# Zero matmuls between the first loads and the first scores of a block-sparse attention kernel

## The chip, the cores and the metric

The kernel runs on one core of a Trainium2 chip. The metric is the device time of one execution in microseconds (us). The core has five engines that are used here, each with its own instruction queue that it works through in order: TensorE (PE in the profile; its weight loads are listed apart as PEld), VectorE (DVE), ScalarE (ACT), GpSimd (POOL) and SyncE (SP), which issues most DMAs. [...]

## The reference

Attention with a block mask, and a two-layer network behind it. Batch 4, 8 heads, 768 positions, head size 64; the mask has blocks of 32.

```python
scores = scale * np.matmul(q, k.transpose(0, 1, 3, 2))
# mask: neighbours, first and last block row and column, 3 sampled blocks per row
scores = np.where(mask, scores, -1000000000.0)
attn = np.exp(scores - np.max(scores, axis=-1, keepdims=True))
attn = attn / (np.sum(attn, axis=-1, keepdims=True) + 1e-09)
x = np.matmul(attn, v)      # then (3072 tokens, 512)
h = x @ w_in                # (512, 2048)
g = h * (1.0 / (1.0 + np.exp(-beta * h)))
out = g @ w_out             # (2048, 512)
```

## The kernel before, in words

Everything is computed in 16-bit floats on TensorE with 32-bit accumulation in PSUM. The heads are taken in pairs (16 pairs, four per batch entry), and a unit is one pair with 256 or 512 query rows. For a unit the kernel needs k and q of the pair, turned so that the head's 64 values lie on the partitions (`kX`, `qX`), and v with a column of ones (`va`). k, q and v come in by DMA as 32-bit floats (`st_k`, `st_q`, `st_v`), are cast by DVE or POOL (`s_k`, `s_q`, `va`), and for the first four pairs turned by TensorE transposes against `identity`; DVE or ACT copies the result out of PSUM to `kX` and `qX`. The first pair's k is loaded in three parts, each cast and turned by itself.

A score step writes a buffer `sc` of two PSUM banks: two heads side by side, in the upper and the lower half of the array's rows, which run at the same time as a pair. In the first four units the mask is added on TensorE: before each pair of score matmuls a pair `sc<-shut_qk,onehot` puts a large negative number where the mask is shut. `shut_qk` is made by ACT out of the mask matmul (`sc<-identity,mask`), which reads `mask`, made by DVE from the sampled blocks. ACT then takes the exponential of the 128x1024 scores (`et<-sc`), in later units DVE multiplies it with a 0/1 mask, and 24 matmuls of 65 columns (`sc<-va,et`) multiply with v. DVE divides by the sum, and the result is turned for the network: `sc<-x,w_in_sb` (h), tanh on ACT (`t_sb`), the gate on DVE (`g`), and products with `w_out_sb`.

There are eight PSUM banks, four double buffers `T["sc"][0..3]`; a buffer of the pool `mm` is one bank of them, numbered 0 to 7, so bank 4 and bank 5 are the two halves of `T["sc"][2]`. The class `Banks` keeps record of who touches which half, and declares instructions of different engines independent where they touch different halves.

The order of all work is written out in `STEPS`: each word is a node's number, a letter for its engine (P TensorE, A ScalarE, D VectorE, G GpSimd, S SyncE) and the slots of the buffers that it takes. `in_steps` (line 157) turns the text into the list `seq`, and the loop at the end of the kernel emits one node after the other; instructions of one engine are queued in that order. The words that matter here: `11S0`, `19S`, `23S` load the three parts of the first k, `12G0` casts the first part, `13P0` turns it (two transposes into bank 0); `25P1`, `17P2` and `21P3` turn the third part, the first q and the second part; `1P4` is the mask matmul into bank 4, `9P0` the transpose of beta, `2A` makes `shut_qk`, `80P3`, `82P2` and `84P1` are the three score steps of unit 0, `81A0`, `83A1`, `85A2` their exponentials. `91P2`, `93P3` and `95P2` are the score steps of unit 1, `86P1` the product with v of unit 0. `54D0` and `50D3` cast q and k of the fourth pair (unit 3), `56A` copies its `qX`.

Before the list begins, `emit_first` sets up constants (among them `warm`, 512 columns of zeros in the buffer that later holds `g`), and ends with `emit_warm(4)`: four matmuls of 512 columns of zeros against zeros, whose result nobody reads. In the profile they stand under line 297; nearly everything else that is emitted through the recording helper stands under line 180.

## Time and profile before

| | |
|---|---|
| median of 3 runs | 271.65 us (271.62 to 271.89) |
| profiled execution | 270.99 us, of which the span from first to last instruction is 269.2 |
| TensorE busy | 257.1 us, 96% of the span |
| VectorE, ScalarE, GpSimd busy | 224.5, 212.6, 24.9 us |
| moved by DMA | 36.67 MB, mean 136 GB/s; some 290 GB/s between 4 and 18 us |

A line of the timeline reads: start in us from the start of the span, duration of the group in us, engine, source line, operation, output and input by the program's names, shapes, number of instructions, and in brackets the idle time of the engine before it and what ended that. Matmuls overlap, and their durations hold the way through the array, so the time that a matmul costs is read from the distance between starts. The chain lists, back from the last instruction, what released each step; shown here in order of time, with start, duration and what it was.

### The profile page before, as it was taken

The numbers are of one execution on the slowest core, as the hardware profiler recorded it, in microseconds if no ns is written. First come the engines' busy times: TensorE is split into PE (matmuls) and PEld (weight loads), VectorE is DVE, ScalarE is ACT, GpSimd is POOL, SyncE is SP. The second block draws the span as 40 slices with busy tenths as digits, with TensorE's granted clock in tenths as the row PEclk, the third lists the DMA queues.
The fourth block names the chain that finished last, engine by engine and source line by source line (L and its number), as shares of the span: only waits on it lengthen the run. The fifth ranks groups of instructions, "written<-read, shape, count | busy, mean of one in ns | idle before, by whom it ended". The sixth has DMA issues, their size and how long they took to land.

```text
span 269.2 us, 6710 instructions
## 1 busy us (share of the span) xinstructions
PE 257.1 (96%) x2719; PEld 163.0 (61%) x2719; DVE 224.5 (83%) x480; ACT 212.6 (79%) x288; POOL 24.9 (9%) x39
## 2 busy tenths in 40 slices
PE   4899799999999999999999999999999999999993
PEld 1576565554453755447776547755467885568883
DVE  6364599889999898989999899878999896898381
ACT  1779999889999796988798699888769678774231
POOL 4170001001110000000021001611000000000000
PEclk9999999999999999999999999999999999999999
DMA  6999996589955487973663079865006010220042
GB/s 183 292 260 213 210 225 186 120 206 227 237 149 150 125 205 143 194 178 105 180 158 57 0 205 225 151 170 46 0 4 195 4 22 2 88 97 2 2 156 78
DMA packets 72881, 36.67 MB, mean 136 GB/s; under 512 B 29828, under 2 KB 68756, under 8 KB 72852
## 3 DMA queue, kind: packets, MB, share of 16 engines
q1 hardware_dynamic: 69600, 32.06, 50.1%
q0 software_dynamic: 3136, 4.19, 8.8%
q8 instruction: 21, 0.34, 0.6%
q14 instruction: 8, 0.07, 0.1%
q10 hardware_dynamic: 116, 0.01, 0.0%
HBM read 27.27 MB, written 6.29 MB: 125 GB/s over the span
## 4 chain that ended last, share of the span: by engine, by line
PE 86%; ACT 5%; DVE 5%; issue 1%; DMA 1%; SPq 1%; POOL 0%; DVEq 0%; ACTq 0%
PE sc L180 86%; ACT et L180 4%; DVE et L180 2%; DVE g L180 1%; DMA st_k<-in_k_dram 1%; ACT t_sb L180 1%; SPq L478 1%; DVE qX L180 0%; DVE kX L180 0%; ACT shut_qk L180 0%; DVE s_k L180 0%; POOL s_k L504 0%; ACT osb L180 0%; ACT qX L180 0%; DVE recip L180 0%
## 5 line engine op out<-in xcount | busy, mean ns | idle before, releaser
L180 ACT ACTIVATE et<-sc 128x1024 f16<-128x1024 f32 x144 | 141.6, 1057 | 17.8 <-PE sc L180 17.1
L180 PE MATMUL sc<-x,w_in_sb 128*128 128x512 f16 (+1 forms) x448 | 90.0, 349 | 0.7 <-DVE g L180 0.7
L180 ACT ACTIVATE t_sb<-sc,beta_c_sb 128x512 f16<-128x512 f32 (+1 forms) x112 | 68.5, 681 | 16.9 <-PE sc L180 15.3
L180 DVE TENSOR_TENSOR et<-et,mask 128x960 f16<-128x960 f16 (+1 forms) x132 | 80.2, 638 | 1.5 <-ACT et L180 1.4
L180 DVE SCALAR_TENSOR_TENSOR g<-t_sb,sc 128x512 f16<-128x512 f16 (+1 forms) x112 | 64.5, 603 | 11.0 <-ACT t_sb L180 10.5
L180 PEld LDWEIGHTS <-w_in_sb 128*128 128x128 f16 x448 | 41.7, 98 | 38.0 <-issue 5.6
L180 PE MATMUL sc<-w_out_sb,g 128*128 128x256 f16 (+1 forms) x384 | 59.0, 300 | 0.0
L180 PEld LDWEIGHTS <-g 128*128 128x128 f16 x456 | 42.0, 98 | 18.9 <-issue 7.0
L180 PE MATMUL sc<-qX,kX 64*128 64x256 f16 (+1 forms) x384 | 47.9, 333 | 2.9 <-ACT et L180 1.4
L180 PEld LDWEIGHTS <-et 128*128 128x128 f16 x1152 | 41.8, 98 | 9.1 <-issue 4.5
L180 PE MATMUL sc<-va,et 128*128 128x65 f16 x1152 | 44.3, 194 | 0.1
L180 PEld LDWEIGHTS <-kX 64*128 64x128 f16 x384 | 17.1, 96 | 22.3 <-issue 17.3
L180 DVE TENSOR_TENSOR xst<-sc,recip 128x256 f16<-128x256 f32 x48 | 19.6, 414 | 0.4
L180 ACT COPY osb<-sc 128x512 f32<-128x512 f32 (+1 forms) x20 | 11.0, 558 | 11.1 <-PE sc L180 11.1
L180 PE MATMUL sc<-w_mix,s 128*128 128x256 f16 x144 | 17.9, 273 | 0.0
L504 POOL CAST s_k<-st_k 128x768 f16<-128x768 f32 (+1 forms) x6 | 7.8, 1308 | 93.4 <-DMA st_k<-in_k_dram 93.4
L180 DVE TENSOR_TENSOR osb<-osb,sc 128x512 f32<-128x512 f32 (+1 forms) x15 | 9.5, 631 | 6.9 <-issue 4.5
L180 DVE RECIPROCAL recip<-sc 128x4 f32<-128x4 f32 x48 | 8.5, 176 | 8.0 <-PE sc L180 7.6
L180 PEld LDWEIGHTS <-s 128*128 128x128 f16 x144 | 13.4, 98 | 2.8 <-issue 1.1
L180 PE MATMUL sc<-w_mix,g 128*128 128x256 f16 x72 | 9.4, 273 | 0.0
L504 POOL CAST s_q<-st_q 128x768 f16<-128x768 f32 (+2 forms) x8 | 6.4, 804 | 22.1 <-DMA st_q<-in_q_dram 22.1
L180 PE MATMUL sc<-shut_qk,onehot 64*128 64x256 f16 x48 | 7.6, 329 | 0.5 <-ACT shut_qk L180 0.5
(65 smaller groups left out, 103.5 us busy)
## 6 DMA issues: line engine op xcount, KB each, us to landing
st_v<-in_v_dram SPq DMA_DIRECT2D x16, 384.0 KB, 4.7
out_dram<-osb SPq DMA_DIRECT2D x24, 256.0 KB, 2.4
st_k<-in_k_dram SPq DMA_DIRECT2D x15, 384.0 KB, 4.5
st_q<-in_q_dram SPq DMA_DIRECT2D x12, 384.0 KB, 4.7
w_in_sb<-in_moe_w_in_dram POOLq DMA_DIRECT2D x2, 1024.0 KB, 12.3
w_out_sb<-in_moe_w_out_dram POOLq DMA_DIRECT2D x2, 1024.0 KB, 21.5
st_q<-in_q_dram SPq DMA_DIRECT2D x12, 128.0 KB, 5.4
st_k<-in_k_dram SPq DMA_DIRECT2D x3, 128.0 KB, 2.7
```

The source lines that it names most:

```text
L180: r = f(*a, **kw)
L478: nc.sync.dma_start(out=o[:, g::NG], in_=hg[:, g::NG])
L504: e(out=at(dst)[:, :, :, 0:D] if nm == "v" else by_chunk(dst, lo, hi), in_=src)
```

## The change

Forty zero matmuls of 64 columns are put into the written order, 33 behind `13P0` and 7 behind `9P0`, and the ones at the start become five instead of four. A new kind of word, `33W7`, means 33 zero matmuls into bank 7; `7W5` means seven into bank 5. Each is a matmul of `warm[:, 0:128]` as weights and `warm[:, 0:64]` as the moving operand, with a weight load of its own; the result is read by nobody. The five at the start also go to bank 7 instead of bank 0. The emission of a word `W` is recorded in `Banks` as an access to its bank by TensorE. The next users are `80P3`, which takes banks 6 and 7, and `82P2`, which takes banks 4 and 5; both begin with matmuls that overwrite them.

```diff
-11S0 15S0 19S 23S 27S0 29S1 12G0 33S1 13P0 16D0 37S1 20D 0D 39S2 24G 43S2 25P1 17P2 14D0 21P3
-1P4 9P0 2A 3A 18A 28D0 22A 80P3 26A 47S0 82P2 81A0 49S3 84P1 30D1 53S0 4P1 10D 34G1 83A1 35P0
+11S0 15S0 19S 23S 27S0 29S1 12G0 33S1 13P0 33W7 16D0 37S1 20D 0D 39S2 24G 43S2 25P1 17P2 14D0 21P3
+1P4 9P0 7W5 2A 3A 18A 28D0 22A 80P3 26A 47S0 82P2 81A0 49S3 84P1 30D1 53S0 4P1 10D 34G1 83A1 35P0
...
     for step in STEPS.split():
+        if "W" in step:
+            seq.append(tuple(int(x) for x in step.split("W")))
+            continue
...
-    def emit_warm(n):
+    def emit_zeros(n, bank, w):
         for _ in range(n):
-            nc.tensor.matmul(T["sc"][0][:, 0, :], lhsT=warm[:, 0:P], rhs=warm,
-                             start=True, stop=True)
+            pe.matmul(T["sc"][bank // 2][:, bank % 2, 0:w], lhsT=warm[:, 0:P],
+                      rhs=warm[:, 0:w], start=True, stop=True)
...
-        emit_warm(4)
+        emit_zeros(5, 7, 512)
...
         for n in seq:
             log.clear()
+            if isinstance(n, tuple):
+                emit_zeros(*n, P // 2)
+                banks.access(list(log), "PE", n[1:], True)
+                continue
```

## The prediction

> **What bounds the kernel now.** The first view is the page: its busy table, its slices, then the chain in order of time.

> ```profile
> span 269.2 us, 6710 instructions
> PE 257.1 (96%) x2719; PEld 163.0 (61%) x2719; DVE 224.5 (83%) x480; ACT 212.6 (79%) x288; POOL 24.9 (9%) x39
> ...
> PEclk9999999999999999999999999999999999999999
> ```

> ```profile
> 5.33 0.41 POOL s_k L504
> ...
> 5.79 0.96 PE sc L180 x7
> ...
> 6.77 0.50 ACT shut_qk L180
> ...
> 7.32 4.01 PE sc L180 x35
> ...
> 11.41 0.56 DVE kX L180
> ...
> 12.22 6.71 PE sc L180 x104
> ...
> 19.62 0.37 ACT qX L180
> 19.99 1.82 ACT et L180 x2
> ...
> 60.19 204.85 PE sc L180 x2098
> ```

> From 60.19 us TensorE alone carries the chain to the end, so what the head saves before that arrives at the end one for one, unless a load holds it up. Between 20 and 50 the chain is ScalarE's, then VectorE's. The head, 5.3 to 19, is TensorE again, and there the timeline shows something that PEclk does not: this row prints full speed from the start, but the starts of the matmuls say otherwise.

> ```profile
> 1.19 1.89 PE L297 MATMUL sc<-g 128*128 128x512 f16 x4 [1.19 <-DVE g L320]
> 3.46 0.39 PE L180 MATMUL sc<-identity,s_k 128*128 128x128 f16 x2 [0.39 <-POOL s_k L504]
> 5.79 0.39 PE L180 MATMUL sc<-identity,s_k 128*128 128x128 f16 x2 [1.93 <-POOL s_k L504]
> ...
> 14.66 1.34 PE L180 MATMUL sc<-va,et 128*128 128x65 f16 x24
> ```

> ```profile
> 13.24 0.44 PE L180 MATMUL sc<-shut_qk,onehot 64*128 64x256 f16 x2
> 13.46 0.44 PE L180 MATMUL sc<-qX,kX 64*128 64x256 f16 x2
> ...
> 16.27 0.27 PE L180 MATMUL sc<-qX,kX 64*128 64x256 f16 x2
> 16.38 0.27 PE L180 MATMUL sc<-shut_qk,onehot 64*128 64x256 f16 x2
> ...
> 17.48 1.00 PE L180 MATMUL sc<-va,et 128*128 128x65 f16 x24
> ```

> A pair of score matmuls of 256 columns follows the next after 0.215 us at 13.24 and after 0.11 us at 16.27. The 24 matmuls of 65 columns take 14.66 to 15.94 to issue, 53 ns each; the next 24 take 17.48 to 18.32, 35 ns each. TensorE runs at half speed until shortly before 15.94, and at full speed from there. What came just before the change of speed: from 12.22 to 15.94 (3.7 us) it streamed with one gap of 0.16 us. The run of 7.32 to 9.93 (2.6 us) had not sufficed, nor the 1.7 us of the four matmuls at the start.

> **The change, part by part.**

> *A fifth matmul of 512 columns, and bank 7 for bank 0.* The four begin 0.427 us apart, so the fifth streams from about 2.90 to 3.32. The next matmul waits for POOL's cast until 3.46. Cost nothing; cover 0.13 us; beyond it the first transposes move, and the DVE copy that reads them (5.71) still has 1.8 us.

> *33 zero matmuls after the first transposes.* These issue from 3.46 at 0.107 us each, until 3.67. Nearest row for a 64-column matmul that loads weights each time: the 65-column ones at half speed, 53 ns. 33 x 0.053 = 1.76 us: 3.67 to 5.43. The next instruction, the transposes at 5.79, waits for POOL's cast, whose DMA landed at 5.28. Cost nothing, margin 0.36 us. Bounds: at the fast rows' 35 ns they end at 4.8; at the pitch of a 128-column matmul, 107 ns, they end at 7.2 and push everything queued behind on TensorE (six transposes, mask, beta) by 1.4 us. I take 53 ns, since the row differs by one column.

> *Seven zero matmuls between the beta transpose and the first scores.* At 53 ns 0.37 us, at 35 ns 0.25, in an idle time: beta issues at 6.59, the first scores wait for shut_qk until 7.32. Cost nothing, margin some 0.3 us. ACT's shut_qk reads bank 4 of the same double bank while they write bank 5; the program declares the two independent, so it waits for the mask matmul alone, as now. No DMA, SP or POOL instruction is added or moved; no PSUM reader stands before the zeros. The 82 extra instructions of the zeros and their weight loads have no wait of their own.

> *What the zeros do to the speed.* TensorE now streams from 1.19 to 5.43 with one gap of 0.13 us: 4.2 us, longer than the 3.7 us that came before full speed in the row above. By that row it is at full speed from about 5.4 instead of 15.9. Then, as a chain of rows (before in brackets):
> - Six transposes from 5.79 at 0.055 us, mask matmul 6.20 (6.54), shut_qk 6.40 (6.77), ACT's qX copy ends 7.21 (7.58): 0.37 earlier.
> - First scores, four pairs 0.11 apart of which the last three wait for that copy: end 7.74 (8.45), first exponential at 7.78 (8.49): 0.71 earlier. Later unit-0 scores are early enough for ACT.
> - Unit 1: POOL's cast of q still waits for its DMA, 8.75 to 9.15. Eight transposes then end at 9.86 (11.31), two DVE copies of 0.56 and 0.28 at 10.66 (12.17), the scores at 11.19, exponential 11.23 (13.08): 1.85 earlier.
> - Unit 2: k and q landed at 11.41 and 11.89 by the landing marks; DVE casts end 12.20, transposes and the first 24-matmul product follow, unit 1's third exponential starts at 13.96 (16.59): 2.6 earlier.
> - Unit 3: here the loads stop it. Its q was issued at 9.61 and landed at 15.02; its k 14.57.

> ```profile
> 9.61 1.29 SPq L478 DMA_DIRECT2D st_q<-in_q_dram  x1
> ...
> 14.62 0.18 POOL L456 CAST w_in_sb<-st_k 1x1 f16<-1x1 f32 x1 [3.69 <-DMA st_k<-in_k_dram]
> ```

> DVE's cast of that q now starts at 16.85, behind 1.8 us of DVE work that the slow clock delayed; it can start at 15.06, no sooner. From it the path is cast, k cast, turns, kX copy, qX copy at 19.62: 2.77 us now, with POOL issuing the weight loads beside it (15.11 to 18.73). Kept at 2.77, the qX copy starts at 17.83, 1.79 us earlier. If the casts run as fast as elsewhere (0.29 against 0.93) the gain is 2.4; if POOL's stretch slows DVE's copy too (0.82 against 0.56 for a cast in that stretch), 1.5. I take 1.8, the duration shown.

> *Does 1.8 us survive to 60?* From 19.89 ACT runs without a gap (3.00 us busy of every 3 from 21 to 42), so it starts 1.8 earlier. Loads on the way, landing against first use: w_in first half 24.9 against 28.65, second 30.8 against 33.58, the last q 31.55 against a transpose at 35.74, w_out halves 36.0 and 41.5 against 42.12 and 45.48. The tightest leaves 2.8 us, 1.0 after the shift. Next late is that second half of w_in. The casts of the second batch (47.66, 51.7) follow DVE's own order, so they move too.

> Sum: 0 + 0 + 0 - 1.8. The profiled execution took 270.99 us, 1.8 around its span of 269.2; it would take 269.2. The three runs' median lies 0.66 higher, so 271.65 - 1.8 = 269.85.

> [...] The row: 3.7 us of streaming came before full speed, and 4.2 us stand there after the change, so the sum is 269.85. [...]

> **The rivals.**

> *Full speed, but late or interrupted.* Say it comes only at 12.2, or comes at 5.4 and is lost again while TensorE waits for k and q between 8.5 and 12.0 (some 1.4 us of streaming in 3.4, sparser than any full-speed stretch of that length in the trace; the sparsest, 25.9 to 29.3, streams 1.9 us by its starts and columns). From 12.22: scores of unit 1 end 12.71 (13.05), its third exponential starts 15.0, and through DVE the cast of unit 3's q at some 15.5, its qX copy at 18.2: 1.4 us earlier. 270.25.

> *The zeros don't open it.* Either zero operands count for nothing, or the gap at 3.33 breaks the run. For it: the four zero matmuls show no effect. Against: they ran 1.7 us only. All 40 lie in idle time: 271.65.

> *Slower.* Each zero matmul takes as long as its 128-column weight load with no overlap, and full speed does not come. At 107 ns they end at 7.2, transposes, scores and exponentials all 1.4 us late: 273.05. It decides from (5.79 - 3.67) / 33 = 64 ns on. Against it: 53 ns with a weight load for each in the 65-column row. For it: weight loads in the groups last 98 ns.

> **How the numbers follow.** Forecast (full speed by 9 at the latest; unit 3's load then sets the same end) 0.60; late or interrupted 0.17; no effect 0.15; slower 0.08. A measurement here tells 0.2%, 0.54 us, from none. Faster 0.60 + 0.17 = 0.77, same 0.15, slower 0.08. The forecast's own range is 269.2 to 270.2 (2.4 to 1.5 us). The range goes to 268.9 below, where DVE passes unit 3 without any of the delay that the 2.6 us lead meets, and to 271.7 above, taking in no effect.

> **What would show it.** Zeros 53 ns apart, ending near 5.4; transposes at 5.79 at 0.055; score pairs 0.11 apart from the first; first exponential near 7.8; DVE's cast of unit 3's q waiting for its DMA at 15.0; the unbroken ACT stretch from about 18.1; TensorE's last stretch 1.8 earlier. Pairs still 0.215 apart at 7.3 would prove the third case; a transpose at 5.79 that waits for zeros, the fourth. Wrong also if the lead shrinks between 20 and 60: look at the first matmul with w_in's second half.

## The result, and the profile after

The change made the kernel slower: 272.55 us (median of 14 runs, 271.52 to 273.72) against 270.77 us for the kernel before (14 runs, 269.27 to 272.14). The ratio is 1.0069, with a 95% interval of 1.0044 to 1.0094. The forecast was 269.85 us, and faster. The profiled execution took 271.52 us, with a span of 269.6, 0.4 us longer than the span of before.

First the page of the changed kernel: span, busy time, the queue that fetches instructions, and the engines' shares of the chain.

```profile
span 269.6 us, 6792 instructions
PE 256.8 (95%) x2760; PEld 162.7 (60%) x2760; DVE 225.8 (84%) x480; ACT 213.2 (79%) x288; POOL 27.4 (10%) x39
...
q8 instruction: 21, 0.34, 0.6%
...
PE 66%; DVE 12%; DMA 10%; ACT 5%; SPq 4%; issue 2%; DVEq 0%; ACTq 0%
```

In TensorE's row there are 41 more matmuls and 41 more weight loads (x2719 each before): 82 more instructions. The last row is the surprise. Before, one piece of TensorE work carried the chain from 60.19 us to the end, and DMAs held 1% of the chain and VectorE 5%; now DMAs hold 10% and VectorE 12%.

The head, in the timeline of the changed kernel:

```profile
1.19 2.31 PE L183 MATMUL sc<-g 128*128 128x512 f16 x5 [1.19 <-DVE g L323]
3.54 0.40 PE L183 MATMUL sc<-identity,s_k 128*128 128x128 f16 x2
3.72 1.97 PE L183 MATMUL sc<-g 128*128 128x64 f16 x33
5.96 0.29 PE L183 MATMUL sc<-identity,s_k 128*128 128x128 f16 x2 [0.27 <-POOL s_k L507]
...
6.64 0.38 PE L183 MATMUL sc<-g 128*128 128x64 f16 x7
...
7.48 0.28 PE L183 MATMUL sc<-qX,kX 64*128 64x256 f16 x2
7.59 0.28 PE L183 MATMUL sc<-shut_qk,onehot 64*128 64x256 f16 x2
...
11.42 0.28 PE L183 MATMUL sc<-qX,kX 64*128 64x256 f16 x2 [0.70 <-DVE qX L183]
11.53 0.28 PE L183 MATMUL sc<-shut_qk,onehot 64*128 64x256 f16 x2
```

Here the forecast came true. The 33 zeros end where they should, the next transposes still wait for POOL and not for zeros, and score pairs follow one another after 0.11 us from 7.48 on, where they took 0.215 before. TensorE has its full speed from about 6 us (the trace's record of the clock says 6.00), 9.6 us earlier than in the profile of before (15.63).

What became of it is in the chain of the changed kernel (start, duration, what it was):

```profile
10.26 5.87 DMA st_q<-in_q_dram
...
16.16 0.29 DVE s_q L183
...
18.18 0.38 ACT qX L183
...
20.91 1.50 PE sc L183 x30
...
54.82 4.65 DMA qX<-s_q
59.47 0.14 issue
59.60 38.57 PE sc L183 x382
...
104.59 6.15 DMA st_k<-in_k_dram
...
138.61 5.01 DMA x<-xst
143.62 0.05 issue
143.66 88.45 PE sc L183 x962
...
236.86 3.31 DMA x<-xst
```

The `qX` copy of unit 3 ends 1.4 us earlier than before (18.56 against 19.99). At 20.91 the transposes that stood at 21.89 are 0.98 earlier, and TensorE's long stretch begins 0.59 earlier (59.60 against 60.19). Behind 60 us the stretch that was one piece is broken: by a load at 104.59 and two transposing transfers `x<-xst` at 138.61 and 236.86. By the starts of the same matmuls in both profiles TensorE lost 0.2, 0.6 and 0.3 us at the three. The last mixing product (`sc<-w_mix,g`, eight matmuls) begins at 264.45, 0.46 us later than before (263.99). So 1.05 us were lost behind 60 us, where I had priced nothing.

What DMA moved while the last of those transfers was under way, in the changed kernel (236.8 to 240.2 us) and then in the kernel before (236.6 to 239.0):

```profile
q1 hardware_dynamic: 566, 0.13, 19.5%
q8 instruction: 1, 0.02, 2.0%
...
out_dram<-osb SPq DMA_DIRECT2D x2, 256.0 KB, 2.3
x<-xst SPq DMA_TRANSPOSE x1, 3.3
```

```profile
q1 hardware_dynamic: 575, 0.14, 26.9%
...
out_dram<-osb SPq DMA_DIRECT2D x2, 256.0 KB, 2.3
x<-xst SPq DMA_TRANSPOSE x1, 2.3
```

The same transfer takes 2.3 us without, and 3.3 us with a piece of the instruction stream beside it. The DMA engines are busy for a fifth and a quarter of these stretches, so it is not their rate that ran out. The program is fetched: queue q8 brought 21 pieces, 0.34 MB in sum, so 16 KB each. In the trace a piece takes 0.9 to 2.1 us. The 5438 matmuls and weight loads of before over 21 pieces are 259; from the start of the first fetch to that of the last TensorE begins 5034 of them (17.2 to 255.6 us), and 5059 in the changed kernel (12.2 to 251.4), so 252 and 253 for each of the 20 steps. I reckon with 256 instructions a piece, an estimate between these numbers. That the pieces are TensorE's shows in the kernels below with 192 and more extra TensorE instructions: they fetch 22.

### The profile page after: what moved, and what is told of

Read it like the earlier page. It is cut to its first block, busy times and chain, and to the rows that moved or that the text cites. A ratio compares the mean times of both kernels' runs of the same rounds, so it can differ in the third digit from the quotient of the medians.

```text
span 269.6 us, 6792 instructions
## 1 busy us (share of the span) xinstructions
PE 256.8 (95%) x2760; PEld 162.7 (60%) x2760; DVE 225.8 (84%) x480; ACT 213.2 (79%) x288; POOL 27.4 (10%) x39
## 4 chain that ended last, share of the span: by engine, by line
PE 66%; DVE 12%; DMA 10%; ACT 5%; SPq 4%; issue 2%; DVEq 0%; ACTq 0%
PE sc L183 66%; DVE g L183 4%; DVE et L183 3%; ACT et L183 3%; DMA x<-xst 3%; DMA st_k<-in_k_dram 2%; DMA st_q<-in_q_dram 2%; SPq L478 2%; DMA qX<-s_q 2%; SPq L481 2%; ACT t_sb L183 1%; DVE s_q L183 1%; DMA out_dram<-osb 1%; DVE xst L183 1%; DVE s_k L183 1%
## 5 line engine op out<-in xcount | busy, mean ns | idle before, releaser
L183 DVE TENSOR_TENSOR et<-et,mask 128x960 f16<-128x960 f16 (+1 forms) x132 | 81.4, 649 | 1.5 <-ACT et L183 1.4
L183 ACT ACTIVATE t_sb<-sc,beta_c_sb 128x512 f16<-128x512 f32 (+1 forms) x112 | 68.1, 664 | 17.2 <-PE sc L183 15.7
L183 PEld LDWEIGHTS <-g 128*128 128x128 f16 x501 | 44.7, 100 | 20.9 <-issue 7.7
L183 PE MATMUL sc<-qX,kX 64*128 64x256 f16 (+1 forms) x384 | 46.0, 326 | 3.5 <-ACT et L183 1.4
L507 POOL CAST s_k<-st_k 128x768 f16<-128x768 f32 (+1 forms) x6 | 8.6, 1426 | 91.9 <-DVE recip L183 60.8
L507 POOL CAST s_q<-st_q 128x768 f16<-128x768 f32 (+2 forms) x8 | 7.3, 916 | 19.6 <-DVE g L183 10.1
L183 DVE CAST s_k<-st_k 128x768 f16<-128x768 f32 (+1 forms) x12 | 7.1, 588 | 2.5 <-DMA st_k<-in_k_dram 2.5
```

What stands on the lines that cost most here:

```text
L183: r = f(*a, **kw)
L507: e(out=at(dst)[:, :, :, 0:D] if nm == "v" else by_chunk(dst, lo, hi), in_=src)
```

## The experiments

Two theories. **Fetches**: 82 more instructions near the start put every later fetch at an earlier place of the program, where it meets other transfers, and some of these are waited for. Then the time depends on the number of instructions added, modulo these 256 (what is left of it over whole pieces), and not on what they do. **Head**: the loss comes from what the zeros do at the start (streaming, early clock, the first loads, the bank). Then it depends on these.

All the kernels differ from one of the two known ones by words of the written order, or by the number, width or bank of zero matmuls. A zero matmul counts for two instructions, with its weight load.

### The change again, and its parts

The changed kernel once more, without an edit:

> The changed kernel once more, beside the others on one chip, for its times and for a second profile. My theory after the first result: full speed came early as forecast (matmul pairs 0.11 us apart from 7.5 us), the lead of 1 to 2 us at 20 us is real, and it is lost behind 60 us in waits for DMAs that TensorE did not have before (ratio about 1.007 again, TensorE no longer the whole chain behind 60). Rival A: the zero matmuls themselves slow the first loads (k and v of the second pair landing 0.7 to 1.0 us later), and the lead is gone at 20 us in most executions. Rival B: the lost time is a matter of single executions, ratio within 0.2% of 1.

Without the 33 zeros, then without the seven, then without both:

```diff
-... 33S1 13P0 33W7 16D0 ...
+... 33S1 13P0 16D0 ...
```

> Without the 33 zero matmuls behind the first transposes; five at the start and the seven before the first scores stay. If early full speed is what costs time later: the clock opens late again, ratio 1.000 to 1.002. If zeros beside the first loads slow these: also near 1.000, but the loads land as before. If the loss is in the seven or in the five: still 1.005 or more.

```diff
-1P4 9P0 7W5 2A 3A ...
+1P4 9P0 2A 3A ...
```

> Without the seven zero matmuls before the first scores; five and 33 stay. If early full speed costs the time: it still opens near 6 us, ratio 1.005 to 1.009. If the seven hold up the first scores: ratio 1.000 to 1.002.

```diff
-... 33S1 13P0 33W7 16D0 ...
-1P4 9P0 7W5 2A 3A ...
+... 33S1 13P0 16D0 ...
+1P4 9P0 2A 3A ...
```

> Only the five matmuls of 512 columns in bank 7 are left of the change. Every theory that blames the 40 small ones expects 1.000 within 0.002, full speed late (12 to 16 us); 1.005 or more would put the loss on the start of the kernel or on the bank.

Measured against 271.01 us of the kernel before: the change again 272.03 us, 1.0050 [1.0026, 1.0075]; without the 33 zeros 269.47, 0.9960 [0.9933, 0.9986]; without the seven 273.22, 1.0094 [1.0060, 1.0129]; without both 270.70, 1.0001 [0.9976, 1.0025]. Of the parts, the 33 zeros bring the loss. The fifth matmul of 512 columns and the other bank cost nothing, as forecast.

Without the seven, a second thing adds to it. The stretches of that kernel's profile, with TensorE's busy time and the granted clock (the number behind POOL):

```profile
22.58:25.99 3.41, 1.95 (x18) 0.99 (x18) 1.79 (x6) 2.92 (x4) 0.00 (x0) 1.00 1.13 216
25.99:29.40 3.41, 2.69 (x13) 1.36 (x13) 0.81 (x3) 3.13 (x5) 0.00 (x0) 0.50 1.13 216
29.40:32.82 3.42, 3.42 (x18) 2.44 (x17) 1.93 (x5) 2.46 (x5) 0.61 (x1) 0.50 1.21 205
```

After a stretch with little work (TensorE busy for 1.95 of 3.41 us) the clock went back to half for 6.8 us. By the starts of the same matmuls this execution was 0.5 us ahead of the kernel without the 33 at 26.7 us and 1.5 behind it at 40.8: 2.0 us lost. It is a cost of an early clock that is not kept, but not the main one: 20 of the 26 executions of the change show a mean clock of 0.997 to 1.0, and their median is still 272.15 us.

### Instructions or streaming

The 33 zeros of 64 columns become four of 512 (the same columns, 58 instructions fewer); or stay 33, with 2 columns (the same instructions, next to no streaming).

```diff
-... 13P0 33W7 16D0 ...
+... 13P0 4W7 16D0 ...
...
-                emit_zeros(*n, P // 2)
+                emit_zeros(*n, 512 if n[0] == 4 else P // 2)
```

> The 33 zero matmuls of 64 columns become 4 of 512 at the same place: 2048 columns streamed instead of 2112, but 8 instructions instead of 66. If the streaming is what costs (TensorE gets full speed before it has work, runs dry and loses it again): as slow as the change, ratio 1.004 to 1.009. If it is the number of instructions (66 more in TensorE's queue, everything behind shifted against the fetching of instructions): 0.995 to 0.998, as without the 33.

```diff
-                emit_zeros(*n, P // 2)
+                emit_zeros(*n, 2 if n[0] == 33 else P // 2)
```

> The 33 keep their number and their weight loads, but stream 2 columns each instead of 64. Streaming theory: 0.995 to 0.999, as without them. Instruction theory: 1.004 to 1.009. If it is the reading of the weights beside the landing loads: also 1.004 or more.

Against 270.58 us: four wide ones 269.60 us, 0.9960 [0.9938, 0.9983], with the clock open at 5.6 us (and at half again from 12.4 to 15.8); 33 thin ones 272.42, 1.0055 [1.0028, 1.0082], with the clock open at 10.8. So the streaming and the early clock don't cost the time, and 33 instructions that do next to nothing do.

The next pair fills TensorE's idle times between 9 and 28 us with 88 more zeros (176 instructions), with the change and without its 33. It was meant to keep the clock from falling back.

```diff
+... 83A1 16W0 35P0 ... 36D 16W4 91P2 ... 44D2 8W2 41P2 ... 105A7 12W4 55P4 ...
+... 107A8 12W2 113P1 116Aa 6W2 61P2 ... 191Ae 12W1 193P2 ... 189D 6W3 199P2 ...
```

> The whole change, and 88 more zero matmuls at eight places between 9 and 28 us where TensorE runs dry after the change. If full speed that is lost again is the cause: no drop of the clock in the profile, and the ratio comes down from 1.005 to 0.997 or less. If the cost is made behind 60 us or at the first loads: it stays at 1.004 or above.

```diff
-... 33S1 13P0 33W7 16D0 ...
+... 33S1 13P0 16D0 ...
```

> The same fillings without the 33. Without the 33 the ratio was 0.996. If the fillings themselves delay nothing: 0.994 to 0.997. If they hold up the work behind them: 0.998 or more, and then the run with the whole change and the fillings has to be read against this one.

Against the same 270.58: with all 128 zeros 270.28 us, 0.9981 [0.9961, 1.0001]; without the 33 274.39, 1.0118 [1.0091, 1.0145]. Taking 33 zeros away cost 4.1 us here and gained 2.6 in the change itself. I know no story about the head that explains both signs. The count does: 258 extra instructions are, by that estimate, one whole piece and two more, and the fetches fall where they fell before (those from about 60 us on at 59.3, 75.0, 87.8, 95.6, 111.2; before 60.2, 76.1, 89.0, 96.4, 111.9; in the changed kernel 56.1, 75.0, 83.1, 92.5, 107.0).

Four kernels put that to the proof: the filled kernel with its 33 zeros thin; with four wide ones for the 33; the kernel before with eight thin zeros and nothing else but the bank; the filled kernel with seven zeros more.

```diff
 # filled kernel, 33 thin
-                emit_zeros(*n, P // 2)
+                emit_zeros(*n, 2 if n[0] == 33 else P // 2)
```

> The kernel with the change and the 88 filling zeros (0.998 of before when its 33 zeros stream 64 columns), with these 33 streaming 2 columns each: the same 258 extra TensorE instructions as that kernel, but as little streaming at the head as the filled kernel without the 33 (1.012). If the number of instructions ahead of each fetch sets the time: 0.998 (about 270.3 us), and fetches of instructions within 1 us of the filled kernel's. If the streaming or the early clock sets it: 1.012 (about 274).

```diff
 # filled kernel, four wide
-... 13P0 33W7 16D0 ...
+... 13P0 4W7 16D0 ...
...
-                emit_zeros(*n, P // 2)
+                emit_zeros(*n, 512 if n[0] == 4 else P // 2)
```

> The filled kernel with four zero matmuls of 512 columns in the place of the 33 of 64: the same streaming, the same early full speed (first score pairs 0.11 us apart), but 200 extra instructions for 258. If the number of instructions sets the time: as the filled kernel without the 33 (192 extra), 1.010 (some 273.5 us). If streaming sets it: as the filled kernel, 0.998 (270.3).

```diff
 # kernel before
-... 33S1 13P0 16D0 ...
+... 33S1 13P0 8W7 16D0 ...
-        emit_warm(4)
+        emit_zeros(4, 7, 512)
...
+                emit_zeros(*n, 2)
```

> The kernel before with only eight zero matmuls of 2 columns behind the first transposes (its four 512-column zeros stay, in bank 7; no seven zeros): 16 extra instructions and next to no streaming. If the 0.996 of the version with five and seven zeros (16 extra) and of the one with four wide ones (24 extra) comes from where the fetches then fall: 0.996 (269.5 us). If it comes from an earlier full speed or an early start: 1.000 (270.6), since the clock opens as before.

```diff
 # filled kernel
-... 83A1 16W0 35P0
+... 83A1 23W0 35P0
```

> The filled kernel with seven more zeros (16 made 23) in its filling at 20 us: 272 extra instructions, that is one whole fetch of 256 and 16 more, as in the kernel with five and seven zeros (0.996). If the number of instructions modulo 256 sets the time: 0.995 to 0.996 (about 269.5 us). If streaming sets it: as the filled kernel, 0.998 (270.3).

Against 270.22: thin 270.73 us, 1.0016 [0.9993, 1.0038]; four wide 272.29, 1.0063 [1.0036, 1.0091]; eight thin 270.68, 1.0006 [0.9971, 1.0041]; seven more 270.33, 1.0002 [0.9979, 1.0025]. The first two decide for the number of instructions: the same streaming is slow with 200 instructions and not slow with 258, and 258 are not slow without streaming. The other two miss: 16 and 272 extra instructions did not give the 0.996 that I had read out of the earlier kernels with 16 and 24. The number tells which kernels lose; a gain does not follow from it.

### The head of before, and the change's number of instructions

If the head has no part in it, the same number of extra instructions must cost as much when they are added later. To the kernel before, with its head as it was, thin zeros (2 columns) are added in idle times of TensorE:

```diff
 # 42 zeros (84 instructions), 18 to 28 us
+... 105A7 12W4 55P4 ... 107A8 12W2 113P1 116Aa 6W2 61P2 ... 191Ae 6W1 193P2 ... 189D 6W3 199P2 ...
```

> The kernel before, its head untouched, with 42 zero matmuls of 2 columns in TensorE's idle times from 18 to 28 us: 84 extra instructions, as many as the change has (82), but no early clock, nothing before the scores, no change of bank, and the first loads land as before. If it is the place of the instruction fetches behind 60 us that costs the time: 1.004 to 1.006 (some 1.3 us), with the fetches behind 60 us within 1 us of the program places of the changed kernel, and the loss behind 60 us. If the head does it (the first loads, the clock, the zeros in front of the scores): 1.000.

```diff
 # 64 zeros (128 instructions), 16 to 28 us
+... 36D 16W4 91P2 ... 44D2 8W2 41P2 ... 105A7 12W4 55P4 ...
+... 107A8 12W2 113P1 116Aa 6W2 61P2 ... 191Ae 6W1 193P2 ... 189D 4W3 199P2 ...
```

> The same with 64 zeros of 2 columns between 16 and 28 us: 128 extra instructions. If the fetches' places set it: a loss as with 82 to 200 extra instructions, 1.004 to 1.010. If the head does it: 1.000.

```diff
 # 96 zeros (192 instructions), 9 to 28 us
+... 83A1 16W0 35P0 ... 36D 16W4 91P2 ... 44D2 8W2 41P2 ... 105A7 16W4 55P4 ...
+... 107A8 16W2 113P1 116Aa 8W2 61P2 ... 191Ae 10W1 193P2 ... 189D 6W3 199P2 ...
```

> The same with 96 zeros of 2 columns between 9 and 28 us: 192 extra instructions, as in the kernel with the fillings alone. If the fetches' places set it: 1.008 to 1.012, with 1.1 us of it lost between 60 and 74 us and 1.1 us at 171 us. If the head and the early clock of that kernel did it: 1.000 to 1.003.

The last is the change without its 33 zeros again, as above:

> The change without its 33 zeros (five of 512 columns, seven of 64; 16 extra instructions) once more, since its 0.996 of the first time was not reached by two other kernels with 16 more instructions modulo 256 (1.0006 and 1.0002). If it is a real gain of this kernel: 0.995 to 0.998. If it was the scatter of the kernel before, whose medians ran from 270.2 to 271.0 us in three calls: 0.999 to 1.001.

Against 270.07: 42 late zeros 272.86 us, 1.0106 [1.0069, 1.0143]; 64 late zeros 273.39, 1.0128 [1.0095, 1.0162]; 96 late zeros 275.57, 1.0203 [1.0174, 1.0231]; without the 33 zeros again 270.01, 0.9988 [0.9966, 1.0011]. With the head of before the loss is there, and rather larger than in the change. All three lose more than I had expected (up to 1.006, 1.010 and 1.012); why, the runs don't show. The profile of the 96 is of the shortest of their six executions, 272.42 us: it has the 1.1 us near 171 that I expected, and nothing of the 1.1 between 60 and 74. And the 0.996 of the kernel without the 33 did not repeat; that of the four wide ones was not measured again. So no version here is shown to beat the kernel before.

The chain of the kernel with 42 late zeros, and what DMA moved from 136.8 to 143.0 us:

```profile
58.68 38.73 PE sc L183 x382
...
103.82 6.34 DMA st_k<-in_k_dram
...
136.73 6.31 DMA x<-xst
143.03 0.05 issue
143.08 15.22 PE sc L183 x135
```

```profile
q8 instruction: 1, 0.02, 1.2%
...
x<-xst SPq DMA_TRANSPOSE x3, 5.8
```

TensorE's long stretch, begun at 58.68, is broken at the same load as in the changed kernel and at a neighbouring `x<-xst`. In the second profile of the kernel without the 33 zeros, which does not lose, it is one piece:

```profile
59.24 205.09 PE sc L183 x2098
```

### All profiles side by side

The time from the start of that stretch (the first score matmul of unit 9, 60.19 in the profile of before) to the start of the last mixing product, from one profile each:

| extra instructions | mod 256 | kernel | ratio | from 60 to the last product, us |
|---|---|---|---|---|
| 0 | 0 | before | | 203.80 |
| 2 | 2 | five zeros of 512 alone | 1.0001 | 203.96 |
| 258 | 2 | filled | 0.9981 | 203.92 |
| 258 | 2 | filled, 33 thin | 1.0016 | 204.06 |
| 16 | 16 | without the 33, twice | 0.9960, 0.9988 | 203.97, 204.03 |
| 16 | 16 | before, eight thin | 1.0006 | 203.83 |
| 272 | 16 | filled, seven more | 1.0002 | 203.96 |
| 24 | 24 | four wide for the 33 | 0.9960 | 203.99 |
| 68 | 68 | without the seven | 1.0094 | 205.80 |
| 82 | 82 | the change, twice | 1.0069, 1.0050 | 204.85, 205.73 |
| 82 | 82 | 33 thin | 1.0055 | 205.43 |
| 84 | 84 | 42 late | 1.0106 | 206.27 |
| 128 | 128 | 64 late | 1.0128 | 206.49 |
| 192 | 192 | filled without the 33 | 1.0118 | 206.99 |
| 192 | 192 | 96 late | 1.0203 | 206.02 |
| 200 | 200 | filled, four wide | 1.0063 | 205.86 |

With 2 to 24 extra instructions modulo 256, eight profiles of seven kernels need 203.8 to 204.1 us, as before; with 68 to 200, nine profiles need 204.9 to 207.0. Neither clock nor streaming nor place of the zeros sorts them so; the number of instructions does. (With 252 for 256 the two groups are the same; with 259, 258 instructions are one short of a whole piece.)

That the fetch is what slows the transfer, I read from the same transfer across the 18 profiles. 34 transposing transfers (`x<-xst`, `qX<-s_q`, `kX<-s_k`) have at least three profiles with a fetch between issue and landing and three without; the median with a fetch is longer by 0.78 us in the mean, by 1.4 to 1.6 in nine of them, and by under 0.1 in eight. (A long transfer also has more time to meet a fetch. With only the fetches counted that begin in the first 1.5 us after the issue, 16 transfers can be compared, and the mean is still 0.70 us.) The one at 237 us: 2.28 to 2.29 in thirteen profiles without, 2.90 to 3.91 in five with. The one that broke the chain at 138.61: 3.04 to 3.77 without, 4.86 to 5.21 with. Not tried is a kernel with the fetches moved and its instructions unchanged; the link from fetch to landing rests on this comparison, the link from number of instructions to time on the runs.

One piece of the loss takes another way: VectorE. In the changed kernel's repetition, then in the kernel without the 33 zeros, POOL's cast and VectorE's multiplies (timeline):

```profile
166.61 1.29 POOL L507 CAST s_k<-st_k 128x768 f16<-128x768 f32 x1 [2.85 <-DMA st_k<-in_k_dram]
...
166.57 4.18 DVE L183 TENSOR_TENSOR et<-et,mask 128x960 f16<-128x960 f16 x5
```

```profile
166.88 4.33 POOL L507 CAST s_k<-st_k 128x768 f16<-128x768 f32 x1 [4.33 <-DMA st_k<-in_k_dram]
...
165.35 2.92 DVE L183 TENSOR_TENSOR et<-et,mask 128x960 f16<-128x960 f16 x5
```

Either POOL's cast of 1.29 us takes 4.33 and VectorE runs through, or the cast runs at once and the five multiplies take 1.26 us longer. In this pair POOL starts at about the same time, set by its load, and VectorE, some 1.2 us late, gives it the turn. But the load matters too. The kernel with 96 late zeros had lost only 0.2 us between 60 and 166 us, and its VectorE is where it was without the 33; its POOL is 1.3 us earlier:

```profile
159.60 0.84 SPq L478 DMA_DIRECT2D st_k<-in_k_dram  x1
...
165.54 1.11 POOL L507 CAST s_k<-st_k 128x768 f16<-128x768 f32 x1 [3.03 <-DMA st_k<-in_k_dram]
...
165.32 4.17 DVE L183 TENSOR_TENSOR et<-et,mask 128x960 f16<-128x960 f16 x5
```

Without the 33 this load was issued at 159.60 as well, but a fetch that began at 159.5 was beside it, and POOL started at 166.88. In eight of the nine profiles with 68 to 200 extra instructions the cast takes 0.9 to 1.3 us, and TensorE is 1.1 us later behind it (the product with v that stands at 171.78 in the profile of before); none of the eight has a fetch between the issue of the load and POOL's release, 5.6 to 6.2 us. In the changed kernel's own profile and the nine others the cast takes 3.8 to 5.1, and nothing is lost there; the nine others all have a fetch in that time, which is 6.7 to 7.6 us. So a fetch moved away from a load can cost time as well, by a comparison of profiles again: POOL, released earlier, starts at most 0.6 us after the first of the five multiplies and gets the turn (0.7 to 2.0 us after it in the ten). Where it happens it is a large step of the loss, 1.1 of the 1.93 us in the repetition.

Here one does hold up the other: two of the five multiplies take 1.27 us for 0.65, and no single one waits out the whole cast. By what the one holds up the other, these rows don't show.

## Why the prediction was wrong, point by point

**Fifth matmul, bank 7.** Forecast 0; alone they measured 1.0001. Right.

**33 zeros at 53 ns from 3.67, ending at 5.43; seven zeros at no cost.** They ran from 3.72, 33 in some 1.75 us, and delayed nothing that waited behind them on TensorE. Right, and the rival with 107 ns each is out.

**Full speed from 5.4.** It came at 6.0, and between 5.0 and 7.2 us in all seven profiles (of six kernels) that have the five wide zeros and the streaming of the 33; in the kernels without it at 10.2 to 15.8. Right. With that streaming the clock opened early in every one of the seven. Why the opening lies anywhere from 10.2 to 15.8 us in the other kernels, whose starts differ little, the runs don't show. The 15.63 of the profile I worked from was thus a late draw.

**Unit 3 gains 1.8 us.** The cast of its q waited for its load, as forecast, but the load landed at 16.13 and not at 15.02: issued 0.65 later, and 5.87 for 5.41 under way. Part of this is mine to have seen: the first instruction fetch, at 17.18 before, fell to 12.24, into this load. In the nine profiles with their first fetch behind 14.9 us it took 5.3 to 5.5; in the five with it between 11.8 and 12.3, 5.9 to 7.0; in the four with it near 14.0, 5.1 to 7.4. The path behind the cast was 0.75 shorter than the 2.77 I kept, so the `qX` copy came 1.4 earlier.

**"Does 1.8 us survive to 60?"** No. In this pair of profiles 0.98 is left at 21 us and 0.59 at 60. Over all: the seven profiles with an early clock have the transposes of 20.91 at 20.8 in the mean, the other eleven at 21.4; at 60 us they stand at 59.9 and 59.8. What is left at 21 us is lost within the scatter of the loads (19.6 to 22.8), and at 60 there is none. Three kernels with the early clock and without the loss behind 60 measured 0.9960, 0.9981 and 1.0002, where 1.8 us would be 0.993. In three of the seven the clock fell back in a sparse stretch: "comes at 5.4 and is lost again", which I gave to a rival, is here, only later (at 12.4, 18.7 and 26.0 us). What I held for it there was misread: 1.4 us in 3.4 is not sparser than any full-speed stretch, since the kernel before streams 1.3 us from 24.7 to 28.1. The stretch of 25.9 to 29.3 is the sparsest only among those that follow one another every 3.41 us (the length of a half-speed stretch in the kernel with four wide zeros, 12.42 to 15.83) from 15.63 on.

**"No DMA, SP or POOL instruction is added or moved" and "the 82 extra instructions … have no wait of their own".** This is the step that failed, and that turned the sign. The instructions are themselves brought by DMA, and 82 more moved every fetch behind them by a third of a piece. It cost 1.05 us behind 60 in the profile of the change, 1.93 in that of its repetition. No POOL instruction was added either, but in the repetition POOL's cast came before VectorE's multiplies instead of behind them, and that is 1.1 of the 1.93.

**"From 60.19 us TensorE alone carries the chain to the end", "unless a load holds it up".** I followed the loads of w_in, q and w_out, and left out the transposing transfers behind 60 us, since they did not stand in the chain. They had no wait, but I worked out no slack for them either: 1.4 us more at 138.61 and 1.0 at 236.86, and they were in it. The rival that ended slower had the sign and not the cause; its zeros of 107 ns did not occur.

The median of three runs that I started from, 271.65, was also high: 270.77 in 14 runs, these three among them, 270.1 to 271.0 in the later comparisons. This alone would have put the range 0.9 us too high, had the sign been right.

## What to carry to other kernels

Added instructions cost more than their time on the engine here: with 33 zeros of 2 columns in an idle time of TensorE the ratio was 1.0055, without them 0.9960 and 0.9988. Where transfers are waited for, count TensorE's instructions modulo one fetch (252 to 259 by the counts above), and look at which transfers the moved fetches meet. When one resource carries the chain "alone" to the end, work out the slack of each transfer that feeds it before calling it safe; here 1.0 and 1.4 us more in flight were too much. And before a gain under 0.5% is believed in such a kernel, move the code by some other number of instructions without effect: the shift alone cost 0.5 to 2.0% here.
